# Scores as three fp32r terms on 64x128 tiles, and expert work cut into shorter pieces

## The chip, the cores and the metric

The kernel runs on one core of one Trainium2 chip. The metric is the device time of one execution in microseconds (us). Engines are named as in the profile: PE (TensorE), PEld (its weight loads), DVE (VectorE), ACT (ScalarE), POOL (GpSimd), SP (SyncE, which issues most DMAs).

## The reference

Attention with a soft cap on the scores, over 8 batches, 12 heads, 448 positions and head size 64, and behind it one expert layer per batch, applied to the 128 rows with the highest gate score:

```python
scores = cap * np.tanh(scale * q @ k.T / cap)          # per head, 448 x 448
attn = np.exp(scores - max); attn /= attn.sum() + 1e-9
x = (attn @ v), heads joined to rows of 768
gate = x @ w_gate                                       # per batch
top = 128 rows with the highest gate
h = np.maximum(x[top] @ w1, 0)                          # 768 -> 1024
out[top] = x[top] + sigmoid(gate[top]) * (h @ w2)       # 1024 -> 768
```

All data is fp32. The output is x with those rows replaced.

## The kernel before

**Doubles and units.** Four heads of one batch make a "double": 24 doubles in all, three to a batch, numbered d = 0 to 23 by order of work. The 448 keys of a double are cut into three blocks of 128 and a last block of 64. One *score unit* computes the scores of one block of 128 keys for the four heads into `psS`, four PSUM banks that exist once (`scores_mm`, L423): eight fp32 matmuls of 448 columns, each on a 64x64 quarter of the array, four of them side by side. The last blocks of two doubles share one unit, so there are 84 units. A `tanh` (L861) takes the unit from `psS` to SBUF, an `exp` (L868) follows in place. Then a *values step* (`values_mm`, L436) multiplies with v: 28 fp32 matmuls of 65 columns on 128x64 halves of the array for a block of 128 keys, on 64x64 quarters for the last block. Of an fp32 matmul the profile counts two instructions (x16 for one unit, x56 for one values step). After the four values steps of a double DVE takes the two accumulators out (`evac`, L467, L468, L473), which exist once too, so the next double's first values step waits for it. SP stores the rows, DVE forms the gate scores (L502).

**Experts.** After three doubles the batch's rows are ranked (L540 to L622 and around), gathered by POOL, turned (L652), split into a high and a low fp32r part (`split_tasks`, L447 and L664), and multiplied in three terms, high by high, high by low, low by high, with w1 (L711, 36 matmuls of 512 columns) and w2 (L748, 48 of 384 columns), all on the full 128x128 array. w1 and w2 themselves are loaded and split into such parts on DVE early on (`weights_proc`, L361 and L364).

**The order of work.** Every engine's instructions are written in an order that a planner works out while the program is built: `Sim` and `Front` keep a clock per engine, prices per task and a priority, and place each task where it could start. On the chip each engine runs its list in order and waits at semaphores. `Front.policy` chooses PE's next piece among "F" (expert and selection work, full array), "Q" (a score unit) and "V" (a values step). An F piece may run as long as `self.left`, which is at most `MOST` = 6000 ns; `due` holds it back until `LEAST` = 2000 ns have gathered; `RESERVE` = 42000 ns of expert work are kept for the time behind the last values step. The rings `K.q`, `K.k`, `K.v` (three slots each) and `K.xn` (three) limit how far loads and outputs run ahead. At the start `load_flag` runs `WARM` matmuls on PE before the first score unit.

Of the kernel before, what the change touches and what calls it, by code (L numbers as in the profile page):

```python
# [16 lines left out]
P = 128  # L17
HD = 64
CAP_FAST = 40.0
EPS = 1e-9  # L20
WARM = 4
# [6 lines left out]
QUARTER, TALL, FULL = range(3)  # L28
SWITCH, AFTER = 100, 45
MARGIN = 150  # L30
RESERVE = 42000
LEAST, MOST = 2000, 6000
PATIENCE = 150
NEAR, LEAD = 60, 3
VISIBLE = {"PE": 230, "DVE": 120, "ACT": 110, "POOL": 150, "SP": 0}
# [180 lines left out]
def allocate(tc, K):  # L216
# [8 lines left out]
    K.wr = t("wr", [P, P], F32R)  # L225
# [29 lines left out]
    K.sg = [t(f"sg{i}", [P, S]) for i in range(2)]  # L255
# [7 lines left out]
    K.xs = Ring([(t("xh", [P, K.ND, P], F32R), t("xl", [P, K.ND, P], F32R))])  # L263
# [5 lines left out]
    K.banks = Ring([bank(tc, K.stack, c, [P, 512]) for c in "TH"])  # L269

# [17 lines left out]
def load_flag(tc, K, cap):  # L288
# [4 lines left out]
    nc.vector.tensor_copy(K.wr, K.ident)  # L293
# [44 lines left out]
def weights_proc(tc, K, w1, w2):  # L338
# [5 lines left out]
    def load(n):  # L344
        nm, w, i, m = parts[n]
        def emit(t):
            at = t.slots[0].obj
            t.tile = at if n % 3 == 0 else K.work.tile([P, 1024], F32, tag=at, name="stage")
            nc.sync.dma_start(t.tile[:, :m], w[i * P:(i + 1) * P, :])

        return Task("SP", 500, emit,
            deps=[K.warmed], take=[K.stages[n % 3]], refs=[2], lag=m * 4 * P / 170, prio=9, kind="wload")
# [31 lines left out]
class Double:  # L384

    def __init__(self, K, d):
        self.d = d
        self.b, self.grp = divmod(d, K.NG)
        self.P, self.pslot = {}, {}
        self.units = list(range(K.NCH))  # L390
        if d % 2:
            self.units = self.units[-1:] + self.units[:-1]
        self.exp = [Event() for _ in self.units]
# [3 lines left out]
    def load(self, tc, K, sim, nm):  # L397
        src, ring = {"q": (K.qd, K.q), "k": (K.kd, K.k), "v": (K.vd, K.v)}[nm]
        ev = sim.add(Task("SP", 700, lambda t: tc.nc.sync.dma_start(t.slots[0].obj, src[self.d]),
                          take=[ring], refs=[K.NCH], lag=2600, prio=1, kind="load"))  # L400
# [7 lines left out]


# [5 lines left out]
def scores_mm(tc, K, D, c, i):  # L415
    k, q = D.at("k"), D.at("q")
    full = K.NCH - 1
# [34 lines left out]
def output_proc(tc, K, D):  # L452
# [24 lines left out]
    for r in range(2):  # L477
# [11 lines left out]
                           reads=[slot], lag=2300, prio=0, kind="store"))]  # L489
# [5 lines left out]
    for c in range(NCH):  # L495
        def score(t, c=c):
            if c < full:
                x, g = slot.obj[:, c, :], K.wg[:, cols]
            else:
# [6 lines left out]
                                 reads=[slot if c < full else tail], prio=3, kind="score")))  # L506
# [11 lines left out]
def select_proc(tc, K, b):  # L518
# [43 lines left out]
    for c in range(NCH):  # L562
# [15 lines left out]
        todo.append(sim.add(Task("DVE", 598, greater, deps=r, reads=[rs, sc], prio=2,  # L578
                                 kind="greater")))
        todo.append(sim.add(Task("DVE", 270 + 130 * c, ties, deps=r, reads=[rs, sc], prio=2,  # L580
# [64 lines left out]
def split_tasks(tc, K, src, at, pair, i0, w, M, dep, reads, take, prio, kind):  # L645
# [12 lines left out]
    if take:  # L658
        pair.append(t.slots[1])
    hi, lo = pair[0].obj  # L660
# [140 lines left out]
class Front:  # L801

    def __init__(self, tc, K, Ds):
# [5 lines left out]
        for D in Ds:  # L809
            whole = [[(D, c)] for c in range(full)]  # L810
            if D.d % 2:
                self.work += [[(Ds[D.d - 1], full), (D, full)]] + whole
            else:
                self.work += whole
# [12 lines left out]
    def score_est(self):  # L827
# [4 lines left out]
        for D, _ in self.work[self.u]:  # L832
            for l in (D.q, D.k):
# [8 lines left out]
    def score_task(self):  # L842
# [3 lines left out]
        reads = [x.slots[0] for D, _ in two for x in (D.q, D.k)]  # L846
# [7 lines left out]
        task = Task("PE", 1498, emit, shape=QUARTER, reads=reads, kind="scores")  # L854
# [23 lines left out]
        return task  # L878

# [40 lines left out]
    def best(self, t, shapes):  # L920
# [3 lines left out]
        for task in sim.pend["PE"]:  # L924
            if task.kind in ("scores", "values") or task.shape not in shapes:
                continue
            if task.kind == "open" and K.open >= (2 if K.tail else 1):
# [19 lines left out]
    def policy(self):  # L947
# [13 lines left out]
        shapes = {"F": FULL, "Q": QUARTER, "V": vs}  # L961
# [5 lines left out]
        two = self.second_value(t)  # L967
        if seg == "F":
            order = "FQV" if self.left > 0 or K.open else "QVF"
# [306 lines left out]
```

## Time and profile before

| | |
|---|---|
| time, median of 3 runs | 475.83 us (475.59 to 476.88) |
| the profiled execution | 476.31 us, of which the span shown is 474.6 us |
| PE, DVE, ACT busy | 457.0, 203.6, 311.0 us |
| mean granted clock | 0.995 |
| last values step ends, last expert matmul starts | 421.96 us, 467.50 us |

The span runs from the first to the last instruction, and what lies around it is 1.7 us. A busy time of PE counts a matmul until its modelled end, so lengths are better read from one piece's start to the next one's. PEclk is the clock granted, as a share of 2.4 GHz.

### The profile page before, as it was taken

What the parts mean: (1) busy time and instruction counts of PE and PEld (TensorE: products, weight loads), DVE (VectorE), ACT (ScalarE), POOL (GpSimd) and SP (SyncE); (2) the same over time, 40 slices, a digit from 0 to 9 for tenths busy, and PEclk for the clock granted to TensorE, in tenths of its full rate; (3) what the DMA queues carried; (4) which work ended last, traced back from release to release, by engine and by line L of the source; (5) the groups of instructions that cost most, each with busy time, mean ns of one, the idle gap of its engine ahead of it and who ended that gap; (6) DMA issues with size and microseconds to landing.
All of it is one profiled execution on the core that took longest, in us unless ns stands there. A gap on an engine that the chain in (4) does not pass through costs nothing.

```text
span 474.6 us, 16684 instructions
## 1 busy us (share of the span) xinstructions
PE 457.0 (96%) x7600; PEld 333.1 (70%) x7600; DVE 203.6 (43%) x710; ACT 311.0 (66%) x197; POOL 22.8 (5%) x53
## 2 busy tenths in 40 slices
PE   6999998999999999999999999999999999999994
PEld 3556656667657777667776877668766777698984
DVE  1074466539324912464314642266131453447321
ACT  3989989866998747686676537768666677630010
POOL 2000001000000010000100010000100000001000
PEclk9999999999999999999999999999999999999998
DMA  7965676544535234423432243333532203110101
GB/s 232 355 197 202 189 224 201 159 135 152 166 114 179 81 112 125 146 80 104 166 111 83 79 134 103 123 104 97 175 113 78 83 17 90 42 41 35 35 34 39
DMA packets 31887, 58.54 MB, mean 123 GB/s; under 512 B 9920, under 2 KB 19904, under 8 KB 31808
## 3 DMA queue, kind: packets, MB, share of 16 engines
q1 hardware_dynamic: 30528, 51.10, 33.3%
q0 software_dynamic: 1280, 6.29, 4.2%
q8 instruction: 61, 1.00, 0.9%
q14 instruction: 18, 0.15, 0.1%
HBM read 43.23 MB, written 14.16 MB: 121 GB/s over the span
## 4 chain that ended last, share of the span: by engine, by line
PE 85%; ACT 6%; issue 4%; DVE 3%; DMA 1%; POOL 0%; POOLq 0%; ACTq 0%; DVEq 0%
PE psV L436 27%; PE psS L423 27%; PE psH L711 6%; PE psH L748 5%; PE psT L711 5%; PE psT L748 4%; ACT p L861 4%; ACT p L868 2%; PE psB L748 2%; PE psT L652 2%; PE psH L652 1%; PE psA L748 1%; PE psV L711 1%; PE psD L711 1%; DMA out<-xe,idx 1%
## 5 line engine op out<-in xcount | busy, mean ns | idle before, releaser
L861 ACT ACTIVATE p<-psS,sc 128x1792 f32<-128x1792 f32 x84 | 147.5, 1756 | 83.3 <-PE psS L423 81.1
L436 PEld LDWEIGHTS psV<-v,p 128*64 128x64 f32 (+1 forms) x5376 | 146.8, 137 | 44.1 <-issue 23.4
L436 PE MATMUL psV<-v,p 128*64 128x65 f32 (+1 forms) x5376 | 155.6, 222 | 3.0 <-DVE xt L473 1.6
L423 PE MATMUL psS<-q,k 64*64 64x448 f32 x1344 | 147.1, 553 | 6.0 <-ACT p L861 5.6
L868 ACT ACTIVATE p<-p,capc 128x1792 f32<-128x1792 f32 x84 | 150.5, 1791 | 2.6
L423 PEld LDWEIGHTS psS<-q,k 64*64 64x64 f32 x1344 | 43.4, 133 | 57.5 <-issue 45.6
L467 DVE RECIPROCAL rec<-psV 128x7 f32<-128x7 f32 x48 | 9.6, 200 | 106.1 <-PE psV L436 106.0
L502 DVE CUSTOM_DVE_ANT_0 jk<-xn,wg 128x256 bf16<-128x256 f32 x72 | 30.3, 421 | 1.3
L468 DVE TENSOR_TENSOR xn<-psV,rec 128x384 f32<-128x384 f32 x48 | 26.8, 558 | 1.6
L565 DVE TENSOR_SCALAR_CACHE_REDUCE jk<-row,score 128x448 bf16<-128x448 f32 (+1 forms) x32 | 21.5, 672 | 0.1
L447 DVE CAST hh<-psH 128x512 fp32r<-128x512 f32 x6 | 4.1, 690 | 33.0 <-PE psH L652 32.9
L572 DVE SCALAR_TENSOR_TENSOR jt<-row,score,before 128x128 bf16<-128x128 f32 (+3 forms) x32 | 16.9, 528 | 0.0
L412 POOL MEMSET v<- 128x14 f32 x24 | 4.1, 170 | 258.2 <-DMA v<-in_v 196.2
L447 DVE CAST hh<-psT 128x512 fp32r<-128x512 f32 x6 | 4.1, 690 | 27.0 <-PE psT L652 27.0
L792 POOL DMA_INDIRECT out<-xe,idx x8 | 8.1, 1016 | 129.8 <-DVE xe L764 128.0
L711 PE MATMUL psH<-w1h,xh 128*128 128x512 f32 x48 | 13.4, 411 | 0.0
L473 DVE TENSOR_SCALAR xt<-psV,rec 128x64 f32<-128x64 f32 x48 | 13.2, 275 | 0.0
L724 ACT ACTIVATE hs<-psH 128x512 f32<-128x512 f32 x8 | 4.8, 597 | 12.0 <-PE psH L711 12.0
L711 PE MATMUL psH<-w1h,xl 128*128 128x512 f32 x48 | 12.5, 395 | 0.0
L711 PE MATMUL psH<-w1l,xh 128*128 128x512 f32 x48 | 12.5, 395 | 0.0
L748 PE MATMUL psH<-w2h,hh 128*128 128x384 f32 x48 | 11.3, 350 | 0.0
L636 POOL DMA_INDIRECT xe<-out,idx x8 | 8.2, 1028 | 58.1 <-DVE gt L622 42.8
(183 smaller groups left out, 419.9 us busy)
## 6 DMA issues: line engine op xcount, KB each, us to landing
v<-in_v SPq DMA_DIRECT2D x24, 455.0 KB, 3.3
q<-in_q SPq DMA_DIRECT2D x23, 448.0 KB, 3.5
k<-in_k SPq DMA_DIRECT2D x23, 448.0 KB, 4.3
out<-xn SPq DMA_DIRECT2D x24, 384.0 KB, 3.8
stage<-in_moe_w SPq DMA_DIRECT2D x4, 512.0 KB, 7.8
stage<-in_moe_w SPq DMA_DIRECT2D x5, 384.0 KB, 4.1
out<-xt SPq DMA_DIRECT2D x48, 32.0 KB, 3.4
hs<-in_moe_w SPq DMA_DIRECT2D x3, 384.0 KB, 3.9
```

What stands on the lines that cost most here:

```text
L423: tc.nc.tensor.matmul(K.S4[HALF[half], n, :K.S], lhsT=k[HALF[j], r, at:at + HD], rhs=q[HALF[j], r, :], start=True, stop=True)
L436: tc.nc.tensor.matmul(D.accs[r].obj[HALF[g], i * WIDE:(i + 1) * WIDE], lhsT=p[rows, h, n * HD:(n + 1) * HD], rhs=v[rows, u, :], start=(c = ...
L468: nc.vector.tensor_tensor(slots[0].obj.rearrange("p c (r j d) -> p r j c d", r=2, j=2)[:, r], blocks[:, :2 * full, :K.D].rearrange("p (j c ...
L473: nc.vector.tensor_scalar(slots[1].obj[:, r, :], blocks[:, 2 * full, :K.D], rec[:, 2 * full:], None, op0=ALU.mult)
L502: nc.vector.tensor_tensor_reduce(out=K.jk[:, :x.shape[1]], in0=x, in1=g, scale=1.0, scalar=0.0, op0=ALU.mult, op1=ALU.add, accum_out=part[ ...
L565: nc.vector.tensor_scalar(K.jk[:m], row[:m], score[:m, c:c + 1], None, op0=ALU.is_gt, op1=ALU.add, accum_out=rk.obj[:m, 0, c:c + 1])
L572: nc.vector.scalar_tensor_tensor(out=K.jt[:m, :n], in0=row[:m, :n], scalar=score[:m, c:c + 1], in1=K.before[:m, at:at + n], op0=ALU.is_equ ...
L652: nc.tensor.transpose(pt[:, i, :M], src[:M, (at + i) * P:(at + i + 1) * P], K.ident[:M, :M])
L711: nc.tensor.matmul(ph[:M], lhsT=(xh, xl)[part][:, i, :M], rhs=K.wts[r][:, i, fs], start=(n == 0), stop=(n == len(ops) - 1))
L748: nc.tensor.matmul(bank[0].obj[:M, :HH], lhsT=hp[0].obj[part][:, i, :M], rhs=K.wts[r][:, i, ds_], start=(start and n == 0), stop=(stop and ...
L861: nc.scalar.activation(slot.obj, K.S4[:, :, :K.S], AF.Tanh, scale=K.sc)
L868: nc.scalar.activation(slot.obj, slot.obj, AF.Exp, scale=K.cap)
```

## The change

1. From the fifth double on (`WHOLE` = 4, `D.parts`) the scores of the three blocks of 128 keys are no longer fp32. q and k of such a double are split on DVE into a high fp32r part (a cast, L440) and a low one (a subtraction, L446), as the expert's operands were already, and the unit is three terms (high by high, low q by high k, high q by low k): twelve fp32r matmuls of 448 columns on 64x128 tiles, two heads side by side (L471). That concerns 60 of the 84 units. The last blocks of 64 keys and the first four doubles stay as they were (L481).
2. The rings for q, k and v have two slots and a third that is lent: those of q and k become slots of the low parts after double 2, that of v becomes the place of the expert's `xh`. `K.xn` has two slots. The split operands have two slots each for the high part and one (later two) for the low part.
3. The planner: `LEAST`, `MOST` 1500 and 2200 ns, `RESERVE` 50000 ns, other rules of choice in `policy`, other priorities for gate scores and ranking on DVE, other assumed DMA times.
4. The start: seven fp32 warm-up matmuls, and no others. (The branch for large caps, not taken here, changes in its scratch buffers alone.)

```diff
-WARM = 4
+WARM = 7
-RESERVE = 42000
-LEAST, MOST = 2000, 6000
+RESERVE = 50000
+LEAST, MOST = 1500, 2200
+WHOLE = 4
+PS, PG, PH = 1.1, 1.1, 1.2
...
-    K.q = ring("q", 3, [P, 2, S])
-    K.k = ring("k", 3, [P, 2, S])
-    K.v = ring("v", 3, [P, 2 * K.NS, WIDE])
+    K.q = ring("q", 2, [P, 2, S])
+    K.k = ring("k", 2, [P, 2, S])
+    K.v = ring("v", 2, [P, 2 * K.NS, WIDE])
...
-    K.xn = ring("xn", 3, [P, NCH - 1, 4 * K.D])
+    K.xn = ring("xn", 2, [P, NCH - 1, 4 * K.D])
...
-    for _ in range(WARM):
-        for j in range(2):
-            nc.tensor.matmul(K.banks.slots[j].obj[:, :K.S], lhsT=K.wr[HALF[j]],
-                             rhs=K.wr[HALF[j], :HD].unsqueeze(1).to_broadcast([HD, K.NS, HD]),
-                             start=True, stop=True)
...
+    def split(self, tc, K):
+        nc = tc.nc
+        for nm in "kq":
...
+                nc.vector.tensor_copy(t.slots[0].obj, self.at(nm))
+
+            h = yield Task("DVE", 610, high, deps=[land], take=[K.high[nm], K.low[nm]],
+                refs=[K.NCH - 1] * 2, prio=1.2, kind="high")
...
+            lo = yield Task("DVE", 1070, lambda t, nm=nm: nc.vector.tensor_tensor(
+                self.low[nm].slots[0].obj, self.at(nm), self.high[nm].slots[0].obj.bitcast(F32),
+                op=ALU.subtract), deps=[h], reads=[land.slots[0]], prio=PH, kind="low")
...
 def scores_mm(tc, K, D, c, i):
+    full = K.NCH - 1
+    if D.parts and c < full:
+        (kh, kl), (qh, ql) = ([part[nm].slots[0].obj for part in (D.high, D.low)] for nm in "kq")
+        terms = ((kh, qh), (kh, ql), (kl, qh))
+        for r in range(2):
+            for n, (a, b) in enumerate(terms):
+                for j in range(2):
+                    tc.nc.tensor.matmul(K.S4[:, 2 * r + j, :K.S],
+                                        lhsT=a[HALF[j], r, c * P:(c + 1) * P],
+                                        rhs=b[HALF[j], r, :], start=(n == 0), stop=(n == 2))
+        return
...
         if seg == "F":
-            order = "FQV" if self.left > 0 or K.open else "QVF"
+            order = "FQV" if self.left > 0 else "QVF"
+        elif f and not big and not self.backlog(t, IDLE):
+            order = "VFQ" if seg == "Q" and two else "FVQ" if seg == "Q" else "QFV"
         elif seg == "V":
-            order = "VQF" if self.ahead() < LEAD or not self.due(t) else "VFQ"
+            order = "VQF"
         elif vs == QUARTER or two:
             order = "VFQ"
         else:
-            order = "FVQ" if self.due(t) else "VFQ"
+            order = "FVQ" if big and self.due(t) else "VQF"
```

What moves, at three places. First PE around an expert piece between two score units. Before, the whole first half of an expert's first layer (`xh`, `xl` with `w1h`, `w1l`, into `psT`) stands between a values step (into `psV`) and a score unit (`psS`, of `q` and `k`):

```order
L436 MATMUL psV_132<-v_92,p_94 64x65 x2
L711 MATMUL psT<-w1h,xh 128x512 x6
L711 MATMUL psT<-w1l,xh 128x512 x6
L711 MATMUL psT<-w1h,xl 128x512 x6
L423 MATMUL psS<-q_87,k_90 64x448 x8
L436 MATMUL psV_128<-v_92,p_95 64x65 x2
```

Now ten such matmuls, of two halves, stand between two score units (`qh` and `kh` are high parts, `ql`, `qlent`, `klent`, `kl` low ones):

```order
L471 MATMUL psS<-qh_104,kh_102 128x448 x2
L471 MATMUL psS<-qlent,kh_102 128x448 x2
L471 MATMUL psS<-qh_104,klent 128x448 x2
L771 MATMUL psT<-w1h,xl 128x512 x3
L771 MATMUL psH<-w1h,xh 128x512 x6
L771 MATMUL psH<-w1l,xh 128x512
L471 MATMUL psS<-qh_103,kh_101 128x448 x2
L471 MATMUL psS<-ql_106,kh_101 128x448 x2
L471 MATMUL psS<-qh_103,kl_105 128x448 x2
```

A piece of 18 became one of 10, and a unit of eight matmuls (one row) became one of twelve (three rows with x2, which come twice in a unit). Over the whole list of PE the array's tile shape (64x64, 64x128, 128x64, 128x128) changes 185 times before and 200 times now. Second DVE, around a double's two evacuations (`rec`, `xn`, `xt`). Before, in the early part, the weights' split stands ahead of them:

```order
L361 CAST w1h<-hs 128x1024
L364 TENSOR_TENSOR w1l<-hs,w1h 128x1024
L467 RECIPROCAL rec_104<-psV_128 128x7
L468 TENSOR_TENSOR xn_100<-psV_128,rec_104 128x2x3x64
L473 TENSOR_SCALAR xt_103<-psV_128,rec_104 128x64
L467 RECIPROCAL rec_105<-psV_132 128x7
L468 TENSOR_TENSOR xn_100<-psV_132,rec_105 128x2x3x64
L473 TENSOR_SCALAR xt_103<-psV_132,rec_105 128x64
```

Now, in the middle of the kernel, the split of q and k stands around them, and a `combine` of an expert (`xe`) between them:

```order
L440 CAST kh_101<-k_87 128x896
L446 TENSOR_TENSOR kl_105<-k_87,kh_101 128x896
L525 RECIPROCAL rec_99<-psV_129 128x7
L526 TENSOR_TENSOR xn_94<-psV_129,rec_99 128x2x3x64
L531 TENSOR_SCALAR xt_97<-psV_129,rec_99 128x64
L824 SCALAR_TENSOR_TENSOR xe_115<-psH,gt_120,xe_115 128x384
L525 RECIPROCAL rec_100<-psV_133 128x7
L526 TENSOR_TENSOR xn_94<-psV_133,rec_100 128x2x3x64
L531 TENSOR_SCALAR xt_97<-psV_133,rec_100 128x64
L440 CAST qh_103<-q_85 128x896
```

So DVE has four more instructions per double in its list, and an evacuation can stand behind one of them. Third the end of the attention on PE, behind the last values step. Before:

```order
L436 MATMUL psV_132<-v_93,p_97 64x65 x2
L652 MATMUL psH<-ident,hs 128x128 x4
L652 MATMUL psT<-ident,xe_114 128x128 x3
L748 MATMUL psA<-w2h,hh 128x384 x4
L748 MATMUL psA<-w2l,hh 128x384 x4
L748 MATMUL psA<-w2h,hl 128x384 x4
L748 MATMUL psB<-w2h,hh 128x384 x4
```

Now:

```order
L494 MATMUL psV_133<-v_88,p_93 64x65 x2
L808 MATMUL psT<-w2h,hh 128x384 x3
L808 MATMUL psT<-w2l,hh 128x384 x4
L808 MATMUL psT<-w2h,hl 128x384 x4
L771 MATMUL psH<-w1h,xh 128x512 x6
L771 MATMUL psH<-w1l,xh 128x512 x5
L670 MATMUL psA<-vals_72,sel_110 128x4 x4
L598 MATMUL psB<-score_112,twice 128x1
```

Counted from there to the end of the list, 72 matmuls with w1 and 144 with w2 remain before, 144 and 203 now: about two experts' work more stands behind the attention. The last expert's own sequence is the same in both.

## Rows read from the trace of the kernel before

**Rows 1.** The page's parts 1 and 2: busy time, share of the span and instructions of the engines; then PE's busy share and the granted clock in 40 slices of 11.9 us.

```profile
PE 457.0 (96%) x7600; PEld 333.1 (70%) x7600; DVE 203.6 (43%) x710; ACT 311.0 (66%) x197; POOL 22.8 (5%) x53
...
PE   6999998999999999999999999999999999999994
...
PEclk9999999999999999999999999999999999999998
```

**Rows 2.** Busy time by stretch of the span: the stretch, its length, busy us and instruction count of PE, PEld, DVE, ACT and POOL in this order, granted clock, DMA share, GB/s.

```profile
60.00:94.00 34.00, 31.66 (x683) 20.67 (x678) 21.28 (x72) 30.37 (x19) 1.68 (x3) 1.00 0.61 196
...
119.00:148.00 29.00, 27.25 (x589) 16.91 (x584) 9.57 (x34) 26.92 (x17) 0.12 (x1) 1.00 0.43 141
...
200.00:300.00 100.00, 100.00 (x1616) 73.89 (x1615) 41.74 (x152) 66.40 (x42) 4.56 (x9) 1.00 0.35 110
...
422.00:468.40 46.40, 46.36 (x257) 42.58 (x255) 21.94 (x66) 3.67 (x7) 2.93 (x3) 1.00 0.11 37
```

**Rows 3.** PE in order of time around the piece of the first order excerpt: start us, duration us until the modelled end, operation. x16 is one score unit, x56 one values step.

```profile
346.73 1.74 PE L423 MATMUL psS<-q,k 64*64 64x448 f32 x16
348.40 1.85 PE L436 MATMUL psV<-v,p 128*64 128x65 f32 x56
350.18 0.66 PE L652 MATMUL psH<-ident,hs 128*128 128x128 f32 x4
...
352.43 1.67 PE L711 MATMUL psT<-w1h,xh 128*128 128x512 f32 x6
353.94 1.56 PE L711 MATMUL psT<-w1l,xh 128*128 128x512 f32 x6
355.34 1.56 PE L711 MATMUL psT<-w1h,xl 128*128 128x512 f32 x6
356.84 1.73 PE L423 MATMUL psS<-q,k 64*64 64x448 f32 x16
358.50 3.49 PE L436 MATMUL psV<-v,p 128*64 128x65 f32 x112
361.92 1.73 PE L423 MATMUL psS<-q,k 64*64 64x448 f32 x16
```

**Rows 4.** PE at the start: the warm-up matmuls (the fp32r ones on 64x128 tiles) and the first score unit.

```profile
1.43 2.08 PE L295 MATMUL psH<-ident 128*128 128x128 f32 x8 [1.43 <-POOL ident masks.py:199]
...
4.74 0.57 PE L298 MATMUL psT<-wr 64*128 64x448 f32 x1
4.75 0.57 PE L298 MATMUL psH<-wr 64*128 64x448 f32 x1
5.12 0.57 PE L298 MATMUL psT<-wr 64*128 64x448 f32 x1
...
6.00 3.26 PE L423 MATMUL psS<-q,k 64*64 64x448 f32 x16
```

**Rows 5.** Groups by form on ACT and DVE: line, engine, operation, tiles, partitions x elements and type, count | busy us, mean ns of one | idle before.

```profile
L868 ACT ACTIVATE p<-p,capc 128x1792 f32<-128x1792 f32 x84 | 150.5, 1791 | 2.6
L861 ACT ACTIVATE p<-psS,sc 128x1792 f32<-128x1792 f32 x84 | 147.5, 1756 | 83.3 <-PE psS L423 81.1 <-PE psV L436 1.4
...
L364 DVE TENSOR_TENSOR w1l<-stage,w1h 128x1024 fp32r<-128x1024 f32 x4 | 4.9, 1222 | 0.1
L364 DVE TENSOR_TENSOR w2l<-stage,w2h 128x768 fp32r<-128x768 f32 x5 | 4.8, 953 | 0.1
...
L361 DVE CAST w2h<-stage 128x768 fp32r<-128x768 f32 x5 | 2.8, 553 | 0.0
L361 DVE CAST w1h<-stage 128x1024 fp32r<-128x1024 f32 x4 | 2.7, 684 | 0.0
```

**Rows 6.** PE in the stretch 119 to 148 us: the first row, one of the two values steps of a last block, and the last two rows. Between 119.24 and 147.87 there are eight score units, six values steps of a block of 128 keys and two of a last block.

```profile
119.24 1.73 PE L423 MATMUL psS<-q,k 64*64 64x448 f32 x16
...
139.57 1.05 PE L436 MATMUL psV<-v,p 64*64 64x65 f32 x56
...
146.20 1.73 PE L423 MATMUL psS<-q,k 64*64 64x448 f32 x16
147.87 0.66 PE L652 MATMUL psT<-ident,hs 128*128 128x128 f32 x4
```

**Rows 7.** DVE in the two evacuations of one double: the first and the last of six instructions.

```profile
51.79 0.21 DVE L467 RECIPROCAL rec<-psV 128x7 f32<-128x7 f32 x1 [8.93 <-PE psV L436]
...
53.40 0.28 DVE L473 TENSOR_SCALAR xt<-psV,rec 128x64 f32<-128x64 f32 x1
```

**Rows 8.** PE behind the last values step: seven transposes and the first matmuls with w2.

```profile
421.96 0.66 PE L652 MATMUL psH<-ident,hs 128*128 128x128 f32 x4
422.45 0.49 PE L652 MATMUL psT<-ident,xe 128*128 128x128 f32 x3
422.70 0.94 PE L748 MATMUL psA<-w2h,hh 128*128 128x384 f32 x4
```

**Rows 9.** The first load of q: its issue on SP's queue (start us, duration us; two transfers), and the group of its transfers (count, KB each, median us from issue to landing).

```profile
2.00 1.06 SPq L1098 DMA_DIRECT2D q<-in_q  x2
...
q<-in_q SPq DMA_DIRECT2D x2, 224.0 KB, 3.0
```

More of the change, by code (lines that the diff above doesn't have):

```diff
@@ L262, in allocate @@
     K.gt = ring("gt", 3, [P, 1])
-    K.xs = Ring([(t("xh", [P, K.ND, P], F32R), t("xl", [P, K.ND, P], F32R))])
+    K.xl = t("xl", [P, K.ND, P], F32R)
+    K.v.slots.append(Slot(K.v, K.work.tile([P, 2 * K.NS, WIDE], F32, tag="xh", name="vlent")))
+    K.v.free.append(K.v.slots[-1])
+    K.xs = Ring([])
+    K.xs.slots = K.v.slots[2:]
     K.hs = Ring([t("hs", [P, 1024])], free=False)
@@ L505, in output_proc @@
         todo.append(sim.add(Task("DVE", 470 if c < full else 340, score, deps=out + [K.wg_in],
-                                 reads=[slot if c < full else tail], prio=3, kind="score")))
+                                 reads=[slot if c < full else tail], prio=PS, kind="score")))
     yield todo + stores
@@ L659, in split_tasks @@
         pair.append(t.slots[1])
+        if take[0] is K.xs and not isinstance(t.slots[1].obj, tuple):
+            t.slots[1].obj = (K.work.tile([P, K.ND, P], F32R, tag="xh", name="xh"), K.xl)
     hi, lo = pair[0].obj
@@ L811, in __init__ @@
             if D.d % 2:
-                self.work += [[(Ds[D.d - 1], full), (D, full)]] + whole
-            else:
-                self.work += whole
+                self.work.append([(Ds[D.d - 1], full), (D, full)])
+            self.work += whole
         self.pairs = len(self.work)
@@ L845, in score_task @@
         two = self.work[u]
-        reads = [x.slots[0] for D, _ in two for x in (D.q, D.k)]
+        shape = self.score_shape()
+        reads = [x.slots[0] for D, _ in two
+                 for x in (D.ready(0, K) if shape == WIDTH else (D.q, D.k))]
         def emit(t):
@@ L878, in score_task, with score_shape @@
         return task
+    def score_shape(self):
+        if self.u == self.pairs:
+            return None
+        D, c = self.work[self.u][0]
+        return WIDTH if D.parts and c < self.K.NCH - 1 else QUARTER
     def value_shape(self):
@@ L926, in best @@
                 continue
-            if task.kind == "open" and K.open >= (2 if K.tail else 1):
+            if task.kind == "open" and (K.open >= (2 if K.tail else 1) or not K.tail and
+                                        self.fill_used > self.total - RESERVE):
                 continue
@@ L985, in policy, with backlog @@
                            kind == "F" and seg != "F")
+    def backlog(self, t, within):
+        for task in self.sim.pend["PE"]:
+            if task.kind in ("open", "mm"):
+                r = task.ready()
+                if r is not None and r <= t + within:
+                    return True
+        return False
     def second_value(self, t):
@@ L1079, in fast_path @@
         sim.spawn(output_proc(tc, K, D))
+        if D.parts:
+            sim.spawn(D.split(tc, K))
     K.front = Front(tc, K, Ds)
@@ L1149, in general_path @@
              K.idx, K.gt, K.xs, K.banks] + K.acc + K.stages
-    for r in rings:
+    for r in rings + list(K.high.values()) + list(K.low.values()):
         reset(r)
```

62 lines of the change are left out of this document (46 added, 16 removed).

## The prediction

> **What bounds the kernel now.** I read the page's busy times and slices first: PE is busy for 96% of the span, 9 tenths or more in nearly every slice, at full granted clock; ACT follows with 66%, DVE with 43% [rows 1]. A mean over stages could mislead, so I read the stretches next. From 200 to 300 us PE is busy for 100.00 of 100 us, from 422 to 468.4 for 46.36 of 46.4; from 60 to 94 and from 119 to 148 it isn't, and there ACT is busy for 30.37 of 34 and 26.92 of 29 us [rows 2]. So two things can shorten the time: fewer PE us outside those two stretches, and PE work that fills the second. PE in order of time shows that its pieces follow each other without a gap, so their prices are the differences of starts [rows 3]: a score unit 1.67 (346.73 to 348.40), a values step 1.78 (348.40 to 350.18), two in a row 3.42 (358.50 to 361.92), six matmuls with w1 1.40 (353.94 to 355.34), 1.50 where a score unit follows (355.34 to 356.84).
>
> **The change part by part.** The sum is made against the profiled execution, 476.31 us; the median of the three runs is 0.48 lower.
>
> *The 60 score units.* The old price is 1.67. At the start the same unit is shown with 3.26 us instead of 1.74 [rows 3, 4], so PE ran at half clock there (the granted clock's first slice doesn't show it), and what doubles, the streaming, is about 1.52; some 0.16 is filling and the change of tile shape. The new unit streams twelve times 448 columns on 64x128 tiles. Do two such tiles run side by side? The warm-up matmuls had just this form: psT and psH start 0.01 apart, the next pair 0.38 later [rows 4], and 448 columns at 1.2 GHz take 0.373; so yes, one column per clock. Six rounds, then. At full clock fp32r takes 1.40/6 = 0.233 for 512 columns [rows 3], in proportion 0.204 for 448. New price 6 x 0.204 + 0.16 = 1.38, a gain of 0.29 less the rounding, I take 0.28: 60 x 0.28 = **-16.8**. Ends: 0.187 a round (448 columns at 2.4 GHz, half of the warm-up's 0.373) gives 1.28 and -23; 0.211 a round gives 1.43 and -14. This second end is two weight loads in turn: seven transposes, each with 128 new columns to load, take 0.74 (421.96 to 422.70) [rows 8], so 0.106 for a load at most, 0.211 for the two that a round needs. I take 0.204, since fp32r operands at full clock gave that.
>
> A rule speaks for the slow end. The Trainium skill, "TensorE: Matmul & The Clock Gate", section "LDWEIGHTS (loading the stationary operand)", says that a load's time goes by its columns alone, 128/1.2 = 107 ns, so that a load for 64 rows is no shorter than one for 128. The 0.106 above agrees with it. By it two loads in turn would bound the round; whether the two row halves load together no row at full clock shows.
>
> *Changes of tile shape.* 200 instead of 185, counted in the two orders. One costs 0.10 (1.50 against 1.40) to 0.14 (2 x 1.78 - 3.42) [rows 3], with the first matmul's filling up to 0.16: 15 x 0.15 = **+2.2** (1.5 to 2.4).
>
> *The wait in 119 to 148 us.* Between 119.24 and 147.87 [rows 6] lie 28.6 us; PE's pieces there are eight units at 1.6 to 1.67, six values steps at 1.78 and two of a last block at about 0.93 (busy row 1.05 less the tail): 25.6. So PE waited for 3.0, and eight units at 1.756 + 1.791 of ACT [rows 5] are 28.4: ACT set the pace. In the new order the first expert's first layer, before one piece of 16 and two and one of 18, is laid between seven score units of that time, and the second layer follows at once. The stretch is then bound by PE: **-3.0** (-3 to 0).
>
> *Units that gain nothing.* From 60 to 94 us there was no expert work to lay in, and in the new order nine new units stand before the first expert matmul, most of them with one values step: 1.38 + 1.78 = 3.16 against 3.55 on ACT. Their 9 x 0.28 = 2.5 come back as waits for `tanh`; ACT had 3.6 of the 34 us free [rows 2], so not all: **+2.0** (0 to 2.5). Later on expert pieces stand beside the units, and ACT, with 298 us for 84 units in some 370 us of attention, has room on the whole.
>
> *DVE.* A cast of 128x896 lies between 0.553 and 0.684, so 0.62; a subtraction between 0.953 and 1.222, so 1.09 [rows 5]. Two of each per double are 3.4, for 20 doubles 68: DVE goes from 203.6 to about 272. It hides beside PE as long as DVE is early enough. What is queued behind it are the evacuations, 1.89 for one double (51.79 to 53.68) [rows 7], on which the next double's first values step waits. With a subtraction in front that is 2.98. In the new order the PE work between the last values step of a double and the first of the next is shorter than 2.98 at five of the boundaries from the fourth on: 1.4, 1.4, 1.9, 2.3 and 2.5 us. At worst 1.6 + 1.6 + 1.1 + 0.7 + 0.5 = 5.5, but the first three fall where ACT sets the pace. New also: the units wait for `kl` and `ql`. The split of a double is one double ahead of its use, some 14 us for 3.4 us of work. No row shows such a wait. I take **+2.0** (0 to 8).
>
> *The two-slot rings, and more expert work behind the attention.* 72 more matmuls with w1 and 59 with w2 move behind the last values step, some 27 us; they cost the same there, since PE was busy for 46.36 of 46.4 us in that stage [rows 2]. The last expert's sequence stays. Loads and stores keep their number and size; I cost the shorter rings at nothing beyond the DVE term, which has their bound.
>
> *The start.* The warm-up now ends near 1.43 + 14 x 0.21 = 4.4 (its old eight took 2.08 with the tail) instead of 5.9; the first unit can then start when q has landed, 2.0 to 2.6 plus 3.0 [rows 9], instead of at 6.00: **-0.4** (-0.9 to +1.6, if the clock comes up one unit later).
>
> Sum: -16.8 + 2.2 - 3.0 + 2.0 + 2.0 - 0.4 = -14.0. 476.3 - 14.0 = 462.3, for the median 461.8; I say **462**.
>
> **Rivals.**
> *Weight loads bound the unit.* 1.43 instead of 1.38: 60 x 0.05 = +3, 465. For it: the 0.106. Against: the warm-up's round was the streaming time alone.
> *Streaming at the full clock's rate.* 1.28: -6, 456. For it: the warm-up kept 0.373 to 0.38 exactly. Against: fp32r at full clock was 9% slower than its columns in every expert piece.
> *ACT keeps the pace.* If the short pieces leave PE waiting as before in 119 to 148 us and half as much again elsewhere, the -3.0 goes and +2 comes: 467. For it: 84 units need 298 us of ACT however fast PE is. Against: most new units have two values steps or an expert piece beside them.
> *DVE becomes the bound (slower).* DVE's list is in order. If at each of the 20 split doubles PE waits for one subtraction in front of the evacuation or the low parts, 20 x 1.09 = 21.8 in place of my 2.0: 482. It decides from 0.8 us a double on, (14.0 + 2.0)/20. Against: DVE has some 240 us of work in about 380 us of attention, and it waited for PE, not PE for it.
> *The tiles don't run side by side (slower, too).* 12 x 0.204 + 0.16 = 2.61, 60 x 0.94 = +56: about 535. Rows 4 speak against it.
>
> **How the numbers follow.** My case 0.64 (its own range 458 to 467), weight loads 0.10, streaming rate 0.08, ACT 0.08, DVE 0.08, no overlap 0.02. The range takes in all but the slower cases and the far end of the faster one: 455 to 471. A measurement of this kernel tells about 0.3%, 1.4 us, from no change. Slower by more: 0.02 and most of DVE's 0.08, so 0.08; within it: 0.03, from DVE at about 0.8 us a double; faster: 0.89.
>
> **What would show it.** In the new profile a unit on 64x128 tiles takes 1.28 to 1.43 from its start to the next piece's; PE has no wait for ACT between 119 us and the end of the attention beyond a us or two; the waits for DVE's evacuation and low parts sum to under 8 us; the last values step ends near 381 us, and the stage behind it is some 74 us long. A unit at 1.5 or more, or PE waiting for L446 or L531 at most doubles, would make the prediction wrong; so would a second score unit at half clock several times over.

## The result and the profile after

The changed kernel takes **464.51 us** (median of 4 runs, 463.17 to 466.25), the kernel before 476.36 on the same chip (4 runs, 475.59 to 476.92): a ratio of **0.9755**, 95% interval 0.9717 to 0.9792. The forecast was 462, in a range of 455 to 471. The profiled execution took 464.68 us with a span of 463.0: 11.6 less than the 476.31 of before, where the sum had 14.0.

First the page's busy times and slices, which answer to [rows 1]:

```profile
PE 446.5 (96%) x7358; PEld 363.3 (78%) x7358; DVE 264.6 (57%) x784; ACT 311.1 (67%) x202; POOL 22.1 (5%) x53
...
PE   6999998999999999999999999999999998999994
...
PEclk9999999999999999999999999999999999999998
```

PE still bounds the kernel, with 10.5 us less to do; DVE has 61 us more. PE's row differs from the one of before in one digit: the 8 from 382 to 394 us, which is a wait behind the attention (experiment 6). Then the stretches, with the columns of [rows 2]; the last one is the stage behind the attention:

```profile
60.00:94.00 34.00, 31.75 (x681) 25.88 (x681) 31.25 (x89) 31.29 (x20) 1.37 (x3) 1.00 0.59 195
119.00:148.00 29.00, 29.00 (x594) 24.08 (x590) 16.71 (x48) 24.32 (x16) 0.25 (x2) 1.00 0.40 129
200.00:300.00 100.00, 100.00 (x1803) 82.68 (x1801) 67.34 (x211) 77.90 (x52) 3.08 (x8) 1.00 0.39 124
380.00:457.00 77.00, 75.05 (x403) 67.09 (x401) 29.12 (x80) 7.15 (x14) 6.84 (x7) 1.00 0.13 43
```

Between 119 and 148 us PE now has no gap. From 60 to 94 it still has one, and there DVE is nearly full as well (31.25 of 34, 21.28 before). In the last row, where PE was full before, 2 us are missing.

One new unit, PE in order of time as in [rows 3]; each row is one round on two 64x128 tiles:

```profile
203.15 0.47 PE L471 MATMUL psS<-qh,kh 64*128 64x448 f32 x2
203.46 0.37 PE L471 MATMUL psS<-qlent,kh 64*128 64x448 f32 x2
203.67 0.37 PE L471 MATMUL psS<-qh,klent 64*128 64x448 f32 x2
203.87 0.36 PE L471 MATMUL psS<-qh,kh 64*128 64x448 f32 x2
204.07 0.36 PE L471 MATMUL psS<-qlent,kh 64*128 64x448 f32 x2
204.27 0.37 PE L471 MATMUL psS<-qh,klent 64*128 64x448 f32 x2
204.57 0.43 PE L610 MATMUL psT<-ident,score 128*128 128x128 f32 x2
```

Rounds follow each other after 0.20 us (203.46 to 204.27 is four of them in 0.81). The first takes 0.31 and the way out to the next shape 0.30. So a unit is 1.42 from its start to the next piece's, 0.20 of which is no streaming.

Last the table of waits, PE's rows: who waited for whom, us in total, times, longest.

```profile
PE psS L481 <- ACT p L923: 3.4, 3, 1.9
PE psB L610 <- DVE score L605: 1.7, 1, 1.7
...
PE psV L494 <- DVE xt L531: 1.2, 3, 0.8
...
PE psS L471 <- ACT p L923: 1.1, 2, 0.6
```

PE waits 4.5 us for ACT in front of five score units, 1.2 us for an evacuation in three places (1.6 in three before), never for a split (L440, L446), and once, behind the attention, for the copy of a score.

To set the two kernels against each other I priced every piece of PE at what it takes where PE doesn't wait (old unit 1.67, new 1.42, values step 1.78, and so on, with the changes of shape); what the trace takes beyond that is called wait here, also where the clock was at half and PE not idle. Against the forecast, in us:

| term | forecast | measured | how |
|---|---|---|---|
| 60 units | -16.8 | -14.8 | 60 x (1.665 - 1.418), medians of the starts' differences |
| changes of shape, other pieces | +2.2 | +2.5 | all pieces 438.0 before, 425.7 after, less the row above |
| wait in 119 to 148 us | -3.0 | -2.6 | 3.0 to 0.4 |
| units that gain nothing, 60 to 94 us | +2.0 | +0.4 | 2.7 to 3.1 |
| waits for DVE and the rest of the attention from 14 us on | +2.0 | +0.6 | 5.5 to 6.1 |
| behind the last values step | 0 | +2.7 | 0.3 to 3.0 |
| start, up to the third `tanh` | -0.4 | -0.4 | 16.64 to 16.21 |
| sum | -14.0 | -11.6 | 476.31 to 464.68 |

The sum and the two prices of the first row are firm. How the rest divides hangs on the prices: with medians by piece and by the piece that follows, taken over the profiles of all runs, the pieces differ by 13.9 instead of 12.3, and the waits from 14 us on grow by 2.7 instead of 1.1. So the rows between are good to about 1.5 us.

### The profile page after: what moved, and what is told of

The parts are those of the page before. It is cut to its first block, busy times and chain, and to the rows that moved or that the text cites. A ratio compares the mean times of both kernels' runs of the same rounds, so it can differ in the third digit from the quotient of the medians.

```text
span 463.0 us, 16297 instructions
## 1 busy us (share of the span) xinstructions
PE 446.5 (96%) x7358; PEld 363.3 (78%) x7358; DVE 264.6 (57%) x784; ACT 311.1 (67%) x202; POOL 22.1 (5%) x53
## 4 chain that ended last, share of the span: by engine, by line
PE 79%; issue 10%; ACT 5%; DMA 3%; DVE 2%; SPq 0%; POOL 0%; POOLq 0%; DVEq 0%; ACTq 0%
PE psV L494 27%; PE psS L471 16%; PE psS L481 8%; PE psH L771 6%; PE psT L771 4%; PE psH L808 3%; ACT p L923 3%; PE psT L808 3%; PE psD L808 2%; PE psC L771 2%; PE psV L808 2%; ACT p L930 2%; DMA out<-xe,idx 2%; PE psT L710 1%; PE psA L808 1%
## 5 line engine op out<-in xcount | busy, mean ns | idle before, releaser
L494 PEld LDWEIGHTS psV<-v,p 128*64 128x64 f32 (+1 forms) x5152 | 139.3, 137 | 24.9 <-issue 15.5
L471 PE MATMUL psS<-qh,kh 64*128 64x448 f32 x240 | 50.3, 415 | 1.3 <-ACT p L923 1.1
L481 PE MATMUL psS<-q,k 64*64 64x448 f32 x328 | 37.4, 572 | 3.7 <-ACT p L923 3.4
L440 DVE CAST kh<-k 128x896 fp32r<-128x896 f32 x20 | 12.5, 625 | 41.1 <-DMA k<-in_k 34.4
L471 PEld LDWEIGHTS psS<-qh,kh 64*128 64x128 f32 x240 | 22.6, 184 | 12.2 <-issue 5.2
L481 PEld LDWEIGHTS psS<-q,k 64*64 64x64 f32 x328 | 11.0, 137 | 16.8 <-issue 10.6
L471 PE MATMUL psS<-qh,kl 64*128 64x448 f32 x120 | 22.1, 362 | 0.0
L471 PE MATMUL psS<-ql,kh 64*128 64x448 f32 x120 | 22.1, 362 | 0.0
L471 PE MATMUL psS<-qh,klent 64*128 64x448 f32 x120 | 22.0, 363 | 0.0
L471 PE MATMUL psS<-qlent,kh 64*128 64x448 f32 x120 | 22.0, 362 | 0.0
```

Of the source, the lines that this page charges most:

```text
L440: nc.vector.tensor_copy(t.slots[0].obj, self.at(nm))
L471: tc.nc.tensor.matmul(K.S4[:, 2 * r + j, :K.S], lhsT=a[HALF[j], r, c * P:(c + 1) * P], rhs=b[HALF[j], r, :], start=(n == 0), stop=(n == 2))
L481: tc.nc.tensor.matmul(K.S4[HALF[half], n, :K.S], lhsT=k[HALF[j], r, at:at + HD], rhs=q[HALF[j], r, :], start=True, stop=True)
L494: tc.nc.tensor.matmul(D.accs[r].obj[HALF[g], i * WIDE:(i + 1) * WIDE], lhsT=p[rows, h, n * HD:(n + 1) * HD], rhs=v[rows, u, :], start=(c = ...
```

## The experiments

Diffs are against the changed kernel. Where several runs stood beside the same runs of before on one chip, its median is named once: 476.42 (25 runs) for the first four experiments, 477.17 (11 runs) for the next four, 477.05 (11 runs) for the last three.

**1. The new order without the new units.**

```diff
-WHOLE = 4
+WHOLE = 24
```

> WHOLE = 24: no double is split, all 84 units stay fp32 on 64x64 quarters; planner rules, rings and start as changed. Theory A (the units' price carries the gain): the pieces of PE, counted in its order at the measured prices, sum to 11.4 us more than in the changed kernel, its waits stay: 475 us (473 to 477), no gain over before beyond about 1 us. Theory B (the short expert pieces carry it, the unit form little): the time stays near 466 to 468.

Measured: 480.11 us (479.27 to 482.94), ratio 1.0092 (1.0058 to 1.0125). The pieces of PE sum to 437.1 in its profile, 11.4 more than with the new units, so the time beyond that is wait: 18.0 us against 14.2. Theory A had the pieces right and the waits wrong: its 473 to 477 is missed by 3 us. The short pieces by themselves are worth nothing, they cost 3.7 us. Two of the waits lie in 60 to 94 us:

```profile
75.92 1.74 PE L481 MATMUL psS<-q,k 64*64 64x448 f32 x16
79.50 0.55 PE L710 MATMUL psT<-ident,xe 128*128 128x128 f32 x3 [1.84 <-DMA xe<-out,idx]
79.97 1.04 PE L494 MATMUL psV<-v,p 64*64 64x65 f32 x56
80.95 0.85 PE L710 MATMUL psH<-ident,xe 128*128 128x128 f32 x3
81.73 2.52 PE L481 MATMUL psS<-q,k 64*64 64x448 f32 x12
```

PE stands at the first expert's transposes, since the gather of `xe` hasn't landed, and twelve matmuls of the unit behind it then take 2.52 (sixteen take 1.73 elsewhere); the granted clock of 60 to 94 us is 0.95 in this run, so it fell to half behind that wait, which by itself loses 1.7 us (an estimate, 0.05 of 34 us). The clock isn't the whole cause: two other executions with a mean granted clock of 0.994, that of the changed kernel's profile, still took 479.27 and 479.87.

**2. The new units with the old rules of order.**

```diff
-RESERVE = 50000
-LEAST, MOST = 1500, 2200
+RESERVE = 42000
+LEAST, MOST = 2000, 6000
...
-            order = "FQV" if self.left > 0 else "QVF"
-        elif f and not big and not self.backlog(t, IDLE):
-            order = "VFQ" if seg == "Q" and two else "FVQ" if seg == "Q" else "QFV"
+            order = "FQV" if self.left > 0 or K.open else "QVF"
...
-            order = "VQF"
+            order = "VQF" if self.ahead() < LEAD or not self.due(t) else "VFQ"
...
-            order = "FVQ" if big and self.due(t) else "VQF"
+            order = "FVQ" if self.due(t) else "VFQ"
```

(and the limit on experts opened at once, as before)

> The rules of choice, LEAST, MOST, RESERVE and the limit on opening as before, the new units kept. Pieces of PE sum to 1.2 us more than in the changed kernel. Theory A (long pieces leave score units standing alone with one values step, 3.2 us of PE against 3.55 of ACT, so PE waits for ACT again): 468 to 472 us, with 4 us or more of waits between 119 us and the end of attention. Theory B (the units alone carry the gain and hide nothing): 465 to 466.5, no such waits.

Measured: 472.79 us (469.03 to 474.74), ratio 0.9907 (0.9875 to 0.9939). That is Theory A, 0.8 above its range. The pieces sum to 426.8, the waits to 21.9 instead of 14.2. The rows of PE's waits that the changed kernel doesn't have, or has smaller:

```profile
PE psT L710 <- DMA xe<-out,idx: 3.3, 2, 1.9
PE psS L471 <- ACT p L923: 2.6, 7, 0.6
```

Behind one of these gathers, at 302 us, the clock fell too (0.86 from 296 to 308 us, 1.7 us lost by the same estimate).

So a square of four stands: 476.4 with neither, 480.1 with the pieces alone, 472.8 with the units alone, 464.5 with both, the last three with the new rings and the new start. The parts are not a sum of two gains: -3.6 and +3.7 apart, -11.9 together. Faster units leave PE waiting for ACT and for gathers unless expert work is laid between them in small portions; the small portions without faster units only move waits.

**3. Each matmul of a unit cut into two of 224 columns.**

```diff
+            for h in range(2):
+                cols = slice(h * 224, (h + 1) * 224)
...
-                    tc.nc.tensor.matmul(K.S4[:, 2 * r + j, :K.S],
+                        tc.nc.tensor.matmul(K.S4[:, 2 * r + j, cols],
...
-                                        rhs=b[HALF[j], r, :], start=(n == 0), stop=(n == 2))
+                                            rhs=b[HALF[j], r, cols], start=(n == 0),
```

> Each of the twelve matmuls of a new unit cut into two of 224 columns: same columns streamed, twice the weight loads. Theory A (the columns set the round, the loads of the two row halves run together beside them): a unit stays at 1.42 to 1.47, the time at 464 to 468. Theory B (two loads in turn, 0.21 us, set the round): a unit takes 12 x 0.21 + 0.2 = 2.7, the time is about 540. Between the two, 0.106 to 0.21 a round, the unit tells how much of the loads lies side by side.

Measured: 473.53 us (470.64 to 476.33), ratio 0.9935 (0.9903 to 0.9966). PE in order of time in one unit:

```profile
206.74 0.37 PE L473 MATMUL psS<-qh,kh 64*128 64x224 f32 x2
206.94 0.28 PE L473 MATMUL psS<-qlent,kh 64*128 64x224 f32 x2
207.06 0.27 PE L473 MATMUL psS<-qh,klent 64*128 64x224 f32 x2
...
208.06 0.27 PE L473 MATMUL psS<-qh,klent 64*128 64x224 f32 x2
208.26 0.43 PE L613 MATMUL psT<-ident,score 128*128 128x128 f32 x2
```

A round of 224 columns takes 0.112 (206.94 to 208.06 is ten rounds), and it has two weight loads. In turn, at the 0.106 of [rows 8], they would take 0.21, so the loads of the two row halves run together. Nor are they two loads of half the length in turn: the two loads of a round start 0.004 us apart and its two matmuls 0.003 (medians of this trace). That is the question which the prediction left open, and it settles the rival of 1.43: the loads don't bound the round of 448 columns, they are covered twice. The Trainium skill, "TensorE: Matmul & The Clock Gate", section "LDWEIGHTS (loading the stationary operand)", gives a load's time as its columns over 1.2, however many rows, an estimate of 107 ns for 128 columns; the trace agrees for one load (0.112 a round), and shows two of them in that time. The unit lasts 1.52 instead of 1.42, 60 x 0.10 = 6 us of the 9 that the kernel loses; the other 3 the runs don't assign. So Theory A is right on the loads and wrong on the time (464 to 468): a round of half the columns takes 0.112, more than half of 0.203.

**4. Each subtraction of the split done twice, in the same order.**

```diff
-            lo = yield Task("DVE", 1070, lambda t, nm=nm: nc.vector.tensor_tensor(
+            lo = yield Task("DVE", 1070, lambda t, nm=nm: [nc.vector.tensor_tensor(
...
-                op=ALU.subtract), deps=[h], reads=[land.slots[0]], prio=PH, kind="low")
+                op=ALU.subtract) for _ in range(2)], deps=[h], reads=[land.slots[0]], prio=PH, kind="low")
```

> Each low part is computed twice, one after the other, with the planner's order kept: 40 x 1.09 = 43.6 us more on DVE, some 308 in all. Theory A (DVE's work is covered by PE's): up to 4 us longer, 465 to 468.5, by a few waits for the low parts and the evacuations. Theory B (DVE is close to the bound; the 2.5 us missing against the forecast are its waits): 20 x 0.8 us or more, 480 and above.

Measured: 478.36 us (474.38 to 481.34), ratio 1.0043 (1.0014 to 1.0072); the profiled execution, 474.38, is the lowest of the ten. Of some 41 us of added DVE work (305.9 busy against 264.6) 14 come out in the median and 10 in the profile, whose waits are 24.3 against 14.2. Where they come out, by stretches as in [rows 2]:

```profile
60.00:94.00 34.00, 29.57 (x614) 23.95 (x614) 32.93 (x82) 28.07 (x18) 1.43 (x3) 0.95 0.50 159
94.00:119.00 25.00, 22.90 (x426) 18.39 (x426) 20.49 (x69) 17.73 (x11) 1.49 (x3) 0.93 0.49 158
119.00:148.00 29.00, 29.00 (x567) 23.36 (x563) 17.01 (x45) 24.77 (x17) 0.25 (x2) 1.00 0.42 134
200.00:300.00 100.00, 99.23 (x1753) 81.00 (x1751) 77.06 (x212) 76.34 (x50) 3.02 (x8) 1.00 0.38 121
```

The time lies between the two theories (468.5 and 480). From 60 to 119 us DVE also splits the last weights and is nearly full up to 94 us, and PE takes 8.6 + 2.3 us beyond its pieces there (3.1 + 0.2 without the doubling). Two of its rows:

```profile
75.76 0.47 PE L471 MATMUL psS<-qlent,kh 64*128 64x448 f32 x2 [1.75 <-DVE qlent L446]
...
96.08 0.34 PE L494 MATMUL psV<-v,p 128*64 128x65 f32 x4 [1.75 <-POOL v L460]
```

So here PE waits for low parts, 1.75 us and once more 1.2, as it never does in the changed kernel; another 1.75 is for a slot of v, whose tie to DVE's work the trace doesn't show. Behind both rows the clock fell to half: 0.95 of 34 us and 0.93 of 25 lose some 3.4 us (an estimate), nearly half of the 7.6. From 119 us on DVE has room: 10 us more of it in 200 to 300 us cost 2. So DVE's new work is hidden with a margin over most of the attention and with hardly any in the first experts' stretch.

**5. Eight matmuls with the identity behind the first score unit.** Their product isn't used; they only keep PE at work while the first `tanh` runs.

```diff
+            if self.u == 0:
+                for _ in range(8):
+                    nc.tensor.matmul(K.banks.slots[1].obj[:, :P], lhsT=K.ident, rhs=K.ident,
+                                     start=True, stop=True)
```

The reason for it is the start of the changed kernel, PE in order of time:

```profile
4.91 2.52 PE L481 MATMUL psS<-q,k 64*64 64x448 f32 x16
9.36 2.72 PE L481 MATMUL psS<-q,k 64*64 64x448 f32 x16 [1.92 <-ACT p L923]
12.01 2.47 PE L494 MATMUL psV<-v,p 128*64 128x65 f32 x56
14.41 1.73 PE L481 MATMUL psS<-q,k 64*64 64x448 f32 x16
```

and the granted clock (the number behind POOL's) from 10 to 13 us:

```profile
10.00:13.00 3.00, 3.00 (x30) 1.26 (x24) 1.54 (x7) 1.97 (x2) 1.40 (x6) 0.50 1.00 385
```

PE had been idle for 1.92 us, and then stood at 1.2 GHz: the second unit takes 2.72 instead of 1.73 and the first values step 2.47 instead of 1.85.

> Eight fp32 matmuls of the identity (1.7 us, their result unused) behind the first score unit, where PE waits 1.9 us for the first tanh. Theory A (that idle time drops the clock to half, which costs the second unit 1.0 us and the first values step 0.6, and ACT's pace hands it on): the granted clock stays at full from 9 to 14 us, the third tanh starts near 14.8 instead of 16.21, the time falls by 1.4: 463.1 us. Theory B (the clock falls anyway, or what is won early is lost at the next wait): 464.5, unchanged.

Measured: 466.21 us (465.51 to 467.64), ratio 0.9765 (0.9741 to 0.9789). The same stretch of this kernel:

```profile
10.00:13.00 3.00, 2.87 (x66) 1.81 (x60) 1.54 (x7) 2.94 (x2) 1.56 (x7) 1.00 1.00 391
```

The clock stays up, the third `tanh` starts at 15.12 instead of 16.21, and nothing is left of it at the end. That is Theory B: what is won early is lost later. Its waits up to 14 us fall from 1.6 to 0.4; a unit at 28.7 takes 0.7 more (why, the trace doesn't show), and between 94 and 119 us the waits rise from 0.2 to 1.6. Half of that is put down to a row of DVE:

```profile
104.11 1.09 DVE L446 TENSOR_TENSOR kl<-k,kh 128x896 fp32r<-128x896 f32 x1
104.24 1.04 PE L494 MATMUL psV<-v,p 64*64 64x65 f32 x56
...
105.22 0.27 PE L670 MATMUL psH<-vals,sel 128*128 128x4 f32 x1
105.35 0.21 DVE L525 RECIPROCAL rec<-psV 128x7 f32<-128x7 f32 x1
105.59 0.56 DVE L526 TENSOR_TENSOR xn<-psV,rec 128x384 f32<-128x384 f32 x1
...
106.24 0.49 PE L670 MATMUL psH<-vals,sel 128*128 128x4 f32 x3 [0.74 <-DVE xn L526]
```

A subtraction stands in front of an evacuation there, as the prediction's DVE term had it, but it isn't late: it ends at 105.20, before the values step that the evacuation waits for (105.28). What PE waits 0.74 us for is a matmul of the selection, whose operands were written by 103.4. In all three profiles with these matmuls (experiments 5, 8 and 10) it waits 0.7 to 0.8 up to the end of that evacuation's `xn`; in the four others of the same order and work (the changed kernel's two, experiments 6 and 11) it doesn't wait at all. Why, the trace doesn't show.

**6. A fourth slot for `idx` and `gt`.** Behind the attention the changed kernel has a wait that the kernel before hadn't:

```profile
381.44 1.00 POOL L852 DMA_INDIRECT out<-xe,idx  x1 [31.21 <-DVE xe L824]
...
382.41 0.16 DVE L587 TENSOR_TENSOR score<-score,part 128x4 f32<-128x4 f32 x1
385.59 0.16 DVE L678 TENSOR_SCALAR idx<-psA 128x1 int32<-128x1 f32 x1 [3.02 <-DMA out<-xe,idx]
385.93 0.15 DVE L605 COPY score<-psB 128x1 f32<-128x1 f32 x1
```

At 381.44 POOL issues the scatter of an earlier expert, which reads its `idx`. At 382.57 DVE has done what it could. Its next instruction writes `idx` into a ring of three slots and waits until that scatter is through; the copy of another batch's scores is queued behind it, and for that copy PE waits until 386.13 (L610, 1.70 in the table of waits).

```diff
-    K.idx = ring("idx", 3, [P, 1], I32)
-    K.gt = ring("gt", 3, [P, 1])
+    K.idx = ring("idx", 4, [P, 1], I32)
+    K.gt = ring("gt", 4, [P, 1])
```

> Four slots instead of three in the rings of idx and gt. Theory A (behind the attention DVE stands at the instruction that writes idx until the scatter of an earlier expert has landed, and with it the score copy that PE waits for): the waits behind the attention fall from 2.9 us to under 1, the time by about 2: 462.5. Theory B (DVE's own chain is that long): waits and time unchanged, 464.5.

Measured: 464.45 us (463.16 to 464.89), ratio 0.9716 (0.9693 to 0.9739). The wait is gone, its place is taken by the gathers for the last experts, which now stand in PE's table:

```profile
PE psD L710 <- DMA xe<-out,idx: 1.0, 1, 1.0
PE psV L710 <- DMA xe<-out,idx: 0.6, 1, 0.6
```

The waits of the whole stage are 2.7 in this profile, 3.0 without the fourth slot: no gain in the profiled execution (span 463.1), as Theory B had it, though not for its reason; perhaps one in the median.

**7. New units from the seventh double on.**

```diff
-WHOLE = 4
+WHOLE = 6
```

> WHOLE = 6: two doubles more stay fp32, six units. Theory A (units before the first expert work gain nothing, ACT sets the pace there): the pieces sum to 1.3 us more, waits between 60 and 94 us get shorter by as much, DVE has 6.8 us less there; 463.5 to 465.5. Theory B (a new unit gains its 0.24 wherever it stands): 466 or more.

Measured: 466.29 us (463.0 to 468.46), ratio 0.9749 (0.972 to 0.9778). Inconclusive: no difference to the changed kernel that the runs can tell. The profiled execution, 468.46, is the slowest of the six, and one row of PE makes most of that:

```profile
81.34 0.83 PE L710 MATMUL psT<-ident,xe 128*128 128x128 f32 x3 [3.50 <-DMA xe<-out,idx]
```

It is the first expert's gather again, as in experiment 1, late by 3.5 us. The pieces sum to 427.0, 1.3 more; what those six units are worth is less than these runs scatter.

**8. Experiments 5 and 6 together.**

> The filler behind the first unit and the four slots together. Theory A (two separate waits): 464.5 - 1.4 - 2.0 = 461, faster than the kernel before by 3.2%. Theory B (one hides the other): no better than the better of the two.

Measured: 464.19 us (463.43 to 464.35), ratio 0.9716 (0.9692 to 0.974). Theory A's 461 failed; the time is Theory B's, but neither wait hides the other: both go, and others come. In its profile the wait behind the attention is 0.7 (3.0), that up to 14 us 0.4 (1.6); 94 to 119 us has 1.6 (0.2) and 200 to 300 us 1.6 (0.7): 3.5 us taken away, 2.3 come back.

**9 to 11. The changed kernel, both edits, and the slots alone, beside each other on one chip.** Nothing is edited anew.

> The changed kernel itself, unaltered, beside the two versions that follow, on one chip, so that they can be told apart from it. Theory A (the wait behind the attention and the half clock at the start are worth something): this kernel is 0.3% or more above the version with both edits. Theory B (what one wait gives back the next one takes): all three agree within 0.3%. For this kernel 464 to 467 us, a ratio of 0.973 to 0.979 to the kernel before.

> Four slots for idx and gt, and eight fp32 matmuls with the identity behind the first score unit, which serve no result; the rest as in the changed kernel. Theory A: 1.5 to 2.5 us below the changed kernel on this chip (its profile showed 2.2 us less wait behind the attention, 1.2 less up to 14 us and 2.3 more between 94 and 300 us, so 1.1 at least, and the two waits of the start and the end don't come back). Theory B: within 1.4 us of it.

> Four slots for idx and gt, nothing else. Theory A: 0.5 to 1.5 us below the changed kernel, since the wait of 1.7 us for the score's copy is gone. Theory B: within 0.5 us of it, since the gathers behind the attention are late next (1.0 and 0.6 us in the profile).

Measured: the changed kernel 466.39 us (463.23 to 469.01), ratio 0.9789 (0.9754 to 0.9824); both edits 464.64 (463.67 to 466.41), 0.9753 (0.9732 to 0.9774); the slots alone 463.85 (463.61 to 465.62), 0.9745 (0.9726 to 0.9763). The half clock of the start was in neither the first nor the third profile, though neither has the filler. In the first, PE's second unit starts after the same idle time and is short:

```profile
9.24 1.73 PE L481 MATMUL psS<-q,k 64*64 64x448 f32 x16 [1.93 <-ACT p L923]
```

This execution starts like the filler's, has 1.4 us of wait in 94 to 119 us and ends at a span of 462.8, against 463.0 with the half clock. In all five profiles of the new units with a full clock at the start and the same order and DVE work (experiments 5, 8 and 9 to 11) the waits up to 14 us are 0.4, those from 94 to 119 us 1.1 to 1.6; in the two with a half clock (the changed kernel's first one, experiment 6) they are 1.6 to 1.8 and 0.2. So in these seven profiles the start doesn't set the end: what it gains, that stretch takes back. Which wait does it there isn't the same each time (the matmul of the selection of experiment 5, a load of v and rows that the trace puts to no one), and I leave it open.

The slots alone have the lowest median here, and beat the kernel before in both sets of runs. Against the changed kernel they are 2.5 us lower, about what was expected of both edits together, and both edits are 1.75 lower, which the expectation had; but the intervals of the ratios overlap in both cases. The gain is likely and not shown; the range of the single runs is 2.0 us with the fourth slot and 5.8 without it.

## Why the prediction was right

**PE is the bound, and the units are the gain: right.** Taking the new units away alone costs 15.6 us (480.11 against 464.51), and the pieces account for 11.4 of it.

**The tiles run side by side, 0.204 a round: right.** Rounds came 0.203 apart (median), read from an expert's fp32r matmuls at full clock in proportion to the columns. The rival of two weight loads in turn has the right size (1.43) for a wrong reason: experiment 3 shows the loads together in 0.112.

**The step that was mis-sized: "some 0.16 is filling and the change of tile shape".** It measured 0.20: six rounds take 1.22 of 1.42. The 0.16 had come from an old unit at half clock against one at full clock, on 64x64 quarters; the new unit goes into and out of 64x128 tiles. With the rounding of 0.29 to 0.28 that leaves a gain of 0.247 a unit instead of 0.28: 60 x 0.033 = 2.0 us, the shortfall of the table's first row and most of the 2.4 by which sum and profile differ; that the other rows' errors nearly cancel (+0.3, +0.4, -1.6, -1.4, +2.7) is luck.

**The wait in 119 to 148 us goes: right,** 2.6 of 3.0. It isn't the short pieces alone that take it away, though. The same stretch in experiment 1 (short pieces, old units) and in experiment 2 (old rules, new units):

```profile
119.00:148.00 29.00, 27.66 (x581) 20.23 (x573) 14.97 (x57) 22.03 (x15) 1.08 (x2) 1.00 0.41 126
119.00:148.00 29.00, 29.00 (x472) 24.36 (x473) 12.01 (x30) 16.72 (x11) 1.14 (x2) 1.00 0.19 57
```

With short pieces and old units PE still waits there; under the old rules it is full there too, in an order of its own, and waits elsewhere. Over the whole the short pieces are needed: experiment 2 has the same PE work within 1.1 us, and 7.7 us more wait.

**Units that gain nothing: too dear.** The stretch of 60 to 94 us lost 0.4 more than before, not 2.0. ACT had more room than I gave it: it did 0.9 us more in these 34 us than before (31.29 against 30.37 in [rows 2]).

**DVE: right in size of work, too dear in waits.** 264.6 us against a forecast of 272; a cast measured 0.625, a subtraction 1.09, as taken. PE never waits for a low part, and 1.2 us for an evacuation, less than before (1.6). The bound of +8 was not idle, however: 41 us more on DVE cost 10 to 14 (experiment 4), 7.6 of the profile's 10 between 60 and 119 us, some 3.4 of them by the half clock behind waits, which no term had.

**The step that failed: "they cost the same there", of the work that moves behind the attention.** The last values step ends at 378.31 (forecast 381), and the stage behind it takes 78 us up to the last matmul (forecast 74), 32 more than before. 27 of these are the matmuls that were counted; some 2.7 (an estimate from the differences of starts) are 21 transposes and four selection matmuls that moved with them and cost nothing in the sum; about 2.7 are waits that weren't there before, 1.7 of them the one in front of L610. With two experts' more work there, rankings stand in DVE's list beside scatters that haven't landed, and a ring of three, which the change hadn't touched, is late. It isn't the ring alone: with a fourth slot the gathers were late by 1.6 in one profile (experiment 6), and 0.7 of wait was left in another (experiment 8). I looked for it in the rings that were shortened; no row of PE's waits names those.

**The start: right by the sum, by luck in its parts.** The first `tanh` starts 1.8 us earlier (7.55 instead of 9.38), and the half clock behind it takes 1.4 back. I had asked only whether the clock would come up later, not whether it would come up and fall again.

## What to carry to other kernels

Price a piece of TensorE work from its rounds, start to start, and the way into and out of its tile shape apart from that: the rounds carried over to the new shape by columns (0.203 for 448; not down to 224, which took 0.112), the way in and out didn't. When a change makes the bounding engine's pieces shorter, ask in the same breath what is to fill the gaps between them; here faster units alone gave 0.9% and shorter expert pieces alone lost as much, and together they gave 2.5%. And a wait that is removed at the start of a long in-order program, or at one place near its end, has to be followed to the next thing that is late before it is booked as gain.

## What the runs showed of the hardware beyond that

- Weight loads of 128 columns for the two row halves run together: two in 0.112 us a round (experiment 3). Behind 448 columns of fp32r, 0.203, they cost nothing.
- An fp32r round of 448 columns on two 64x128 tiles takes 0.203 at the full clock, 9% more than 448 columns at 2.4 GHz (0.187).
- After 1.92 us of idle time behind the first unit the granted clock was 0.50 from 10 to 13 us in one execution of the changed kernel, and 1.00 after 1.93 us in another. Of the nine profiles of the new start without work in that gap six show a clock of 0.50 to 0.62 there, three 1.00; the three with work in the gap all show 1.00.
- In the middle of four variants the clock fell to half as well, each time behind idle time of PE: 1.75 us (experiment 4, twice), 1.84 (experiment 1), 1.92 (experiment 2) and 3.50 (experiment 7). Behind the changed kernel's 1.70 us in front of L610 it stayed up (1.00 from 380 to 386 us).
- A change of tile shape can be read from the old units alone: one takes 1.664 where a values step on 128x64 halves follows and 1.554 where one on its own 64x64 quarters does (medians over the profiles), so 0.11.
- A gather late by 1.8 and 3.5 us at the first expert, in single executions (experiments 1 and 7), has no counterpart in the profiles of the changed kernel; what delayed it stays open.
